# Two chained mixture-of-experts layers on one core: where the small steps of the second layer stand, four PSUM banks to a group of products, and weight addresses held in registers

## The chip, the core and the metric

The kernel runs on one core of a Trainium2 chip. TensorE (PE) multiplies, VectorE (DVE), ScalarE (ACT) and GpSimd (POOL) do the rest, SyncE (SP) issues most transfers. The metric is the device time of one launch in microseconds. Three runs of the kernel before took 2098.08, 2098.32 and 2103.15 us, so the median is 2098.32 us.

## The reference

Three stages follow each other on 14336 rows of 192 numbers.

```python
# 1: a causal convolution with softmaxed taps, one set of 7 for each of 8 heads of 24 columns
out = np.einsum('hk,bskhg->bshg', w, x_unf)
# 2: first layer, one expert of 8 for each row
expert_idx = np.argmax(x @ w_gate, axis=1)
h = np.maximum(xe @ w1[e], 0.0)             # (192, 1024)
out[mask] = gate_w[mask, None] * (h @ w2[e]) # (1024, 192)
# 3: second layer, two experts of 8 for each row, picked by noisy logits
noisy_logits = logits + np.log1p(np.exp(x @ w_noise)) * noise
out[mask] += top2_w[mask, k, None] * (h @ w2[e])
```

So the first layer puts 14336 rows through an expert, the second 28672. The kernel computes each float32 product as three 16-bit ones (high by high, high by low, low by high).

## The kernel before, in words

**Rows and steps.** The convolution and the gates run for 448 tokens at a time. POOL scatters each finished row into a table in DRAM (`rows1`, then `rows2`) that is ordered by expert. An expert's rows are then worked off in steps. A step is one expert and `t` rows: 1024 (two halves of 512 with the same weights), 512, 256 or 128. How many rows an expert gets is only known on the chip, so the number of steps of each size is fixed beforehand, and a table (`table`, one for each group of steps of one size) gives each step its expert and first row, as numbers that an engine loads into a register (`value_load`). The first layer has 68 steps: 45 of 256 rows, 2 of 512 and 21 of 128. The second has 77: 4 of 512 with their own copy of the second weights (the bridge, `tx`), 19 of 1024 as 38 halves, 7 of 512, 7 of 256 and 21 of 128. They stand in the order of `seq`: within a layer all large ones first, then 256, then 128. Steps share batches of up to 512 rows (`bats`) for their tiles `xT`, `ax`, `y`.

**A step** (`load`, `mm1`, `parts`, `mm2`, `finish`). SP loads 1 MB of first weights (`w1t`, three buffers), the step's rows transposed (`xT`, and for pairs `x3`) and their auxiliary columns (`ax`). `mm1` multiplies: for each of 8 chunks of 128 hidden columns there are four products with 128 contracted rows and one with 64 (192 = 128 + 64, and the low parts). With `st.nb == 2` two chunks in two banks are worked on together, and their two 64-row products run side by side in the upper and the lower half of the array. With `st.nb == 1` the fifth product uses 128 rows as well. `parts` empties a bank: ACT writes the rectified high half of `h`, DVE the low half. `mm2` multiplies `h` by the second weights `w2r` into a bank `py`, 24 products for each 128 rows. The weights are picked by the register `st.re` plus a constant, and the sequencer of PE computes that sum before each product. `finish` scales by the gate on ACT. In the second layer POOL then scatter-adds 128 rows to the output (`add_out`): the adds of one step don't wait for each other, but each waits for those of the step before.

**Order.** `run` goes through `seq`. It puts `mm1` of a step and `mm2` of the step before it in turns: one group of `nb` banks, then as many products of the second kind as keep step. All engines work their instructions in this written order. A planner with its own clocks (`pump`, `clk`) only decides where the other work (convolution, gates, row scatters) falls in between.

In the profile every instruction that goes through a small recording class has line 95.

Of the kernel before, what the change touches and what calls it, by code (L numbers as in the profile page):

```python
# [44 lines left out]
HOP = 0.15  # L45
BRIDGE = 4


# [4 lines left out]
def n_ceil(avail, t):  # L53
    return (avail + E * (t - 1)) // t
# [3 lines left out]
def conv_moe_moe2_kernel(ctx: ExitStack, tc: tile.TileContext, xh, cw, cwb, wg, w11, w21, w2t, w12, w22, out):  # L58
# [574 lines left out]
    def table(g, total):  # L633
# [48 lines left out]
        v.tensor_copy(tb[:, 0:2], val[:, 0:2])  # L682
        v.tensor_scalar(tb[:, 2:3], val[:, 1:2], float(FC * 2 * DG), None, op0=OP.mult)
        dg = L("dg", (P, 2, steps))
# [219 lines left out]
    def load(st):  # L904
# [16 lines left out]
        ins = [q_.dma_start_transpose(st.xT, rows[row, 0:HALF].bitcast(F16))]  # L921
        if st.nb == 2:
            if st.off == 0:
                st.b.x3 = wk.tile([P, 512], F16, name="x3", bufs=3)
            st.x3 = st.b.x3[:, st.off * P:st.off * P + T]
            ins.append(q_.dma_start_transpose(st.x3[:, None, :], rows[row, 32:96].bitcast(F16)))
# [5 lines left out]

    def chunk(st, k):

        n = 512 // st.T
        f, j = divmod(k, n)
        return f // st.nb * n + j + f % st.nb * FC // 2

    def mm1(st, f):


        T, n = st.T, 512 // st.T
        if f == 0:
            st.h = wk.tile([P, 2, 512 * FC // n], F16, name="h", tag="h", bufs=2)
            st.hv = st.h.rearrange("p k (c t) -> p k c t", c=FC)
        if f == st.nb % 2 and not st.g.own:
            st.re = t_.value_load(st.g.tb[st.i:st.i + 1, 2:3], min_val=0, max_val=(E - 1) * FC * 2 * DG)
        st.ph = [ps_h.tile([P, 512], F32, name="ph") for _ in range(st.nb)]
        x = lambda k: st.xT[:, k, :]
        for j in range(n):  # L950
            o = [ph[:, j * T:(j + 1) * T] for ph in st.ph]
            ws = []
            for b in range(st.nb):
                c = chunk(st, (f + b) * n + j)
                w = [st.w[0][:, k * F + c * P:k * F + (c + 1) * P] for k in range(4)]
                t_.matmul(o[b], w[0], x(0), start=True, stop=False)
                t_.matmul(o[b], w[0], x(2), start=False, stop=False)
                t_.matmul(o[b], w[1], x(0), start=False, stop=False)
                t_.matmul(o[b], w[2], x(1), start=False, stop=False)
                ws.append(w[3])  # L960
            if st.nb == 1:
                t_.matmul(o[0], ws[0], x(1), start=False, stop=True)
            else:
                t_.matmul(o[0], ws[0][:64], x(1)[:64], start=False, stop=True)
                t_.matmul(o[1], ws[1][64:], st.x3[64:], start=False, stop=True)

# [11 lines left out]

    w2flat = w2r.rearrange("p e c -> p (e c)")

    def mm2(st, lo, hi):

        for qn in range(lo, hi):
# [5 lines left out]
            hs = slice(s * P, (s + 1) * P)  # L989
            cw = chunk(st, c)  # L990
            if st.g.own:
                w = [st.w[1][:, (2 * cw + k) * D:(2 * cw + k + 1) * D] for k in range(2)]
            else:
                off = st.re + cw * 2 * dd
                w = [w2flat[:, bass.ds(off + k * dd if k else off, dd)] for k in range(2)]
            t_.matmul(py, st.hv[:, 0, c, hs], w[0], start=(c == 0), stop=False)
# [158 lines left out]
    def run(seq):  # L1155
# [12 lines left out]
        for n, st in enumerate(seq + [None]):  # L1168
# [9 lines left out]
            for f in range(0, ns, nb):  # L1178
                ahead(n + 3)
                if st is not None:  # L1180
                    clk["pe"] = max(clk["pe"], emptied[nb - 1])
                    mm1(st, f)
                    if st.g.m and f == ns - nb:
                        ahead(n + 4)
# [22 lines left out]

    def group(m, t, k, last, own, tag):
        g = Step()
        g.m, g.t, g.k, g.last, g.own, g.tag, g.tb, g.bc, g.deps = m, t, k, last, own, tag, None, None, None  # L1210
        for i in range(k):
            w = [None, None]
            for skip in range(0, t, 512):
                st = Step()
                st.g, st.T, st.i, st.skip, st.w, st.first, st.end = g, min(t, 512), i, skip, w, skip == 0, None
                st.nb = 2 if t > P and (m or t == 512) else 1
                S = st.T // P
                if not bats or bats[-1].S + S > 4:
                    bats.append(Batch())
                    bats[-1].S, bats[-1].pads = 0, False  # L1220
                st.b, st.off = bats[-1], bats[-1].S
                st.b.S += S
                st.b.pads |= last
                seq.append(st)
        return g

    def full_groups(m, left, sizes, tag):
# [9 lines left out]
    for k, n in enumerate(EPOCHS):  # L1237
        left, gs = full_groups(0, left + n * G * OT, (512, 256), f"ta{k}")
        if k == len(EPOCHS) - 1:
            gs.append(group(0, P, n_ceil(left, P), True, False, "ta"))  # L1240
        ep_groups.append(gs)
    n1, nb1 = len(seq), len(bats)
    bridge = group(1, 512, BRIDGE, False, True, "tx")
    left, rest = full_groups(1, 2 * N - BRIDGE * 512, (1024, 512, 256), "tb")
    rest.append(group(1, P, n_ceil(left, P), True, False, "tb"))

    def zero_out():
# [111 lines left out]
```

## Time and profile before

| what | value |
|---|---|
| median of three runs | 2098.32 us |
| the profiled execution, with what lies around its span | 2103.14 us |
| its span | 2101.1 us |
| PE busy | 1796.6 us (86%) |
| DVE, ACT, POOL busy | 946.8, 848.5, 834.3 us |
| mean granted clock of PE | 0.910 |

A granted clock of 1.00 is 2.4 GHz, 0.50 is 1.2 GHz. Matmuls are pipelined: one of 512 columns is shown as 0.38 us long while the next one starts much earlier. So a busy PE says little, and the distance from one start to the next is what counts. In a line of the order of time that merges n equal products, that distance is (its length less the length of one) / (n - 1). "Issue" is idle time for which the profile shows no one waited for.

### The profile page before, as it was taken

To read this page: it belongs to the slowest core of one execution; us is meant where nothing else is said; L and a number is where in the kernel's file an instruction comes from. 1 tells how busy PE (TensorE), PEld (TensorE's weight loads), DVE (VectorE), ACT (ScalarE), POOL (GpSimd) and SP (SyncE) were. 2 spreads that over 40 slices of the span, in tenths; PEclk is the share of its full clock that TensorE was granted. 3 is DMA by queue.
4 is the path that set the end of the run, shared out by engine and by line. 5 is a ranking of instruction groups with operands and counts; after the bars stand their busy time and mean duration, and the time that the engine had idled before them with its cause. 6 is when DMAs were issued, how large, how long until landed. Compare 5 with 4: busy or idle time off the path is not lost. (4 is left out here: it accounts for less than half of the span.)

```text
span 2101.1 us, 51695 instructions
## 1 busy us (share of the span) xinstructions
PE 1796.6 (86%) x16031; PEld 1365.3 (65%) x16031; DVE 946.8 (45%) x3508; ACT 848.5 (40%) x1756; POOL 834.3 (40%) x1512
## 2 busy tenths in 40 slices
PE   4778867667868897877789999999999999999993
PEld 3547756556757674766656666666666666667893
DVE  6856644535456574443345433333333333333341
ACT  4745644444334453433333333333333333333331
POOL 1453454545443334353335433333333333343323
PEclk9768988878879898888899999999999999999996
DMA  7868655334458785545698545554554556667792
GB/s 251 281 204 233 205 169 140 109 106 140 144 190 257 225 257 152 163 161 187 192 258 233 102 78 96 85 101 86 88 96 77 102 83 117 116 107 148 203 273 51
DMA packets 320693, 329.04 MB, mean 157 GB/s; under 512 B 230718, under 2 KB 279108, under 8 KB 303296
## 3 DMA queue, kind: packets, MB, share of 16 engines
q1 hardware_dynamic: 258400, 236.98, 40.2%
q0 software_dynamic: 55184, 74.92, 18.3%
q10 hardware_dynamic: 6864, 13.83, 2.0%
q8 instruction: 159, 2.61, 0.5%
q14 instruction: 86, 0.70, 0.1%
HBM read 189.50 MB, written 96.08 MB: 136 GB/s over the span
## 5 line engine op out<-in xcount | busy, mean ns | idle before, releaser
L95 PE MATMUL ph<-xT,w1t 128*128 128x256 f16 (+4 forms) x5568 | 877.0, 303 | 91.4 <-issue 78.7
L95 DVE SCALAR_TENSOR_TENSOR h<-ph,h 128x512 f16<-128x512 f32 x700 | 462.9, 687 | 961.1 <-ACT h L95 899.1
L95 PE MATMUL py<-w2r,h 128*128 x8016 | 813.5, 255 | 75.7 <-issue 74.4
L95 PEld LDWEIGHTS <-h 128*128 128x128 f16 x8400 | 726.2, 100 | 164.7 <-issue 146.8
L95 PEld LDWEIGHTS <-w1t 128*128 128x128 f16 (+1 forms) x5800 | 485.2, 101 | 398.0 <-issue 216.1
L95 ACT ACTIVATE h<-ph 128x512 f16<-128x512 f32 x700 | 392.3, 594 | 682.2 <-PE ph L95 493.7
L95 POOL DMA_INDIRECT out_dram<-y,ax x231 | 361.0, 1563 | 607.4 <-ACT y L95 421.3
L95 POOL DMA_INDIRECT rows<-row,gdi x238 | 237.3, 997 | 214.7 <-issue 189.0
L95 ACT ACTIVATE y<-py,cf 128x192 f32<-128x192 f32 (+1 forms) x350 | 148.6, 424 | 385.0 <-PE py L95 259.7
L95 POOL DMA_INDIRECT rows<-row,di x128 | 125.9, 984 | 152.2 <-DVE di L95 36.9
L95 POOL MEMSET spacer<- 1x1 f32 x613 | 172.4, 281 | 0.1
L95 PE MATMUL ph<-x,w1t 64*128 64x512 f16 (+1 forms) x232 | 87.3, 376 | 0.1
L95 PE MATMUL ph<-x,band 118*112 118x96 f32 x512 | 70.3, 299 | 5.2 <-issue 3.8
L95 PEld LDWEIGHTS ph<-x,band 118*112 118x112 f32 x512 | 66.4, 213 | 7.9 <-issue 5.5
L95 ACT ACTIVATE x<-x,ras 112x192 f32<-112x192 f32 x128 | 49.0, 446 | 19.3 <-DVE rai L95 13.2
L95 POOL CAST row<-gix 128x8 f32<-128x8 uint32 (+1 forms) x30 | 6.9, 229 | 110.0 <-DVE gex L95 47.0
L95 ACT ACTIVATE y<-y,rbs 128x192 f32<-128x192 f32 x119 | 46.5, 445 | 6.9 <-DVE rbs L95 6.9
L95 ACT ACTIVATE rT<-ph 128x672 f16<-128x672 f16 x64 | 43.2, 729 | 15.0 <-PE ph L95 10.7
L95 PE MATMUL ph<-ident,row 112*128 112x112 f16 x384 | 33.3, 245 | 15.4 <-DVE row L95 6.4
L95 PEld LDWEIGHTS <-row 112*128 112x128 f16 x384 | 27.6, 116 | 21.5 <-issue 12.7
L95 DVE TENSOR_TENSOR row<-x,row 112x256 f16<-112x256 f32 x64 | 33.4, 554 | 13.1 <-ACT row L95 12.9
L95 ACT ACTIVATE x<-ph 112x384 f32<-112x384 f32 x64 | 28.2, 480 | 27.0 <-PE ph L95 13.5
(275 smaller groups left out, 1142.6 us busy)
## 6 DMA issues: line engine op xcount, KB each, us to landing
w1t<-w1s SPq DMA_DIRECT2D x126, 1024.0 KB
x<-in_xh_dram ACTq DMA_DIRECT2D x32, 400.0 KB
w1raw<-in_w_dram SPq DMA_DIRECT2D x8, 1536.0 KB
w2raw<-in_w_dram SPq DMA_DIRECT2D x16, 768.0 KB
out_dram<-pads SPq DMA_DIRECT2D x11, 960.0 KB
w1s<-w1raw POOLq DMA_DIRECT2D x16, 512.0 KB
w1s<-whalf SPq DMA_DIRECT2D x16, 512.0 KB
w2tr<-in_w2t_dram POOLq DMA_DIRECT2D x16, 384.0 KB
```

Of the source, the lines that this page charges most:

```text
L95: r = f(*a, **kw)
```

## The change

Four things are changed.

- The second layer's steps of 256 and 128 rows are put into ten batches, and these stand between the large ones (`mixed`). Four large halves come first, and three steps of 512 rows end the program. In the last epoch of the first layer, two steps of 128 and one of 256 take turns (`packed`).
- In the second layer a group of steps with more than 128 rows takes all four banks `ph`: two chunks, then the 64-row products of all four, then the other two chunks. In the first layer the two steps of 512 rows take one bank at a time, and their fifth product uses 128 rows.
- At a step's third product PE loads the expert's offset once and adds 16 constants to it, in registers. Each second product then takes its address from a register.
- The chunks are worked off in plain order.

```diff
--- before.py
+++ after.py
...
         tb = cst.tile([P, 3], I32, name=g.tag + "tb")
         v.tensor_copy(tb[:, 0:2], val[:, 0:2])
-        v.tensor_scalar(tb[:, 2:3], val[:, 1:2], float(FC * 2 * DG), None, op0=OP.mult)
+        v.tensor_scalar(tb[:, 2:3], val[:, 1:2], float(4 * FC * DG), None, op0=OP.mult)
...
-        if st.nb == 2:
-            if st.off == 0:
+        if st.nb == 4:
+            if st.b.x3 is None:
                 st.b.x3 = wk.tile([P, 512], F16, name="x3", bufs=3)
...
     def mm1(st, f):
 
 
@@ -943,26 +938,45 @@
         if f == 0:
             st.h = wk.tile([P, 2, 512 * FC // n], F16, name="h", tag="h", bufs=2)
             st.hv = st.h.rearrange("p k (c t) -> p k c t", c=FC)
-        if f == st.nb % 2 and not st.g.own:
-            st.re = t_.value_load(st.g.tb[st.i:st.i + 1, 2:3], min_val=0, max_val=(E - 1) * FC * 2 * DG)
         st.ph = [ps_h.tile([P, 512], F32, name="ph") for _ in range(st.nb)]
         x = lambda k: st.xT[:, k, :]
+
+        def w(b, j, k):
+            c = (f + b) * n + j
+            return st.w[0][:, k * F + c * P:k * F + (c + 1) * P]
+
+        out_ = lambda b, j: st.ph[b][:, j * T:(j + 1) * T]
+        def whole(b):
+            for j in range(n):
+                o = out_(b, j)
+                first = j == 0 and b < 2
+                t_.matmul(o, w(b, j, 0), x(0), start=first, stop=False, skip_group_check=True)
+                t_.matmul(o, w(b, j, 0), x(2), start=False, stop=False, skip_group_check=True)
+                if f == b == j == 0 and not st.g.own:
+                    addresses(st)
+                t_.matmul(o, w(b, j, 1), x(0), start=False, stop=False, skip_group_check=True)
+                t_.matmul(o, w(b, j, 2), x(1), start=False, stop=b > 1, skip_group_check=True)
+
+        if st.nb == 4:
+            whole(0)
+            whole(1)
+            for b in (0, 2):
+                for j in range(n):
+                    for i, (rows, src) in enumerate(((slice(0, 64), x(1)), (slice(64, P), st.x3))):
+                        t_.matmul(out_(b + i, j), w(b + i, j, 3)[rows], src[rows], start=b == 2 and j == 0,
+                                  stop=b == 0, skip_group_check=True)
+            whole(2)
+            whole(3)
+            return
         for j in range(n):
-            o = [ph[:, j * T:(j + 1) * T] for ph in st.ph]
-            ws = []
-            for b in range(st.nb):
-                c = chunk(st, (f + b) * n + j)
-                w = [st.w[0][:, k * F + c * P:k * F + (c + 1) * P] for k in range(4)]
-                t_.matmul(o[b], w[0], x(0), start=True, stop=False)
-                t_.matmul(o[b], w[0], x(2), start=False, stop=False)
-                t_.matmul(o[b], w[1], x(0), start=False, stop=False)
-                t_.matmul(o[b], w[2], x(1), start=False, stop=False)
-                ws.append(w[3])
-            if st.nb == 1:
-                t_.matmul(o[0], ws[0], x(1), start=False, stop=True)
-            else:
-                t_.matmul(o[0], ws[0][:64], x(1)[:64], start=False, stop=True)
-                t_.matmul(o[1], ws[1][64:], st.x3[64:], start=False, stop=True)
+            o = out_(0, j)
+            t_.matmul(o, w(0, j, 0), x(0), start=True, stop=False)
+            t_.matmul(o, w(0, j, 0), x(2), start=False, stop=False)
+            if f == j == 0 and not st.g.own:
+                addresses(st)
+            t_.matmul(o, w(0, j, 1), x(0), start=False, stop=False)
+            t_.matmul(o, w(0, j, 2), x(1), start=False, stop=False)
+            t_.matmul(o, w(0, j, 3), x(1), start=False, stop=True)
...
-    w2flat = w2r.rearrange("p e c -> p (e c)")
+    w2bytes = w2r.rearrange("p e c -> p (e c)").bitcast(mybir.dt.uint8)
+
+    def addresses(st):
+
+        pe = nc.tensor
+        first = pe.value_load(st.g.tb[st.i:st.i + 1, 2:3], min_val=0, max_val=4 * (E - 1) * FC * DG)
+        step = 2 * (D if st.g.m else DG)
+        st.wr = []
+        for k in range(2 * FC):
+            r = pe.alloc_register(f"w2at{len(addressed)}_{k}")
+            pe.reg_alu(r, first, W2_AT + k * step, op=OP.add)
+            st.wr.append(pe.snap(r, min_val=W2_AT, max_val=W2_AT + 4 * (E - 1) * FC * DG + k * step,
+                                 guaranteed_mod_val=0, out_of_modulus=32))
+        addressed.append(st)
+
+    addressed = []
...
-            cw = chunk(st, c)
+            cw = c
             if st.g.own:
                 w = [st.w[1][:, (2 * cw + k) * D:(2 * cw + k + 1) * D] for k in range(2)]
             else:
-                off = st.re + cw * 2 * dd
-                w = [w2flat[:, bass.ds(off + k * dd if k else off, dd)] for k in range(2)]
+                w = [w2bytes[:, bass.ds(st.wr[2 * cw + k] - W2_AT, 2 * dd)].bitcast(F16) for k in range(2)]
...
-                    clk["pe"] = max(clk["pe"], emptied[nb - 1])
+                    clk["pe"] = max(clk["pe"], emptied[nb // 3])
...
-                st.nb = 2 if t > P and (m or t == 512) else 1
+                st.nb = 4 if m and t > P else 1
...
+    def queue(parts_):
+
+        for st in parts_:
+            S = st.T // P
+            if not bats or bats[-1].S + S > 4 or bats[-1].m != st.g.m:
+                bats.append(Batch())
+                bats[-1].S, bats[-1].pads, bats[-1].m, bats[-1].x3 = 0, False, st.g.m, None
+            st.b, st.off = bats[-1], bats[-1].S
+            st.b.S += S
+            st.b.pads |= st.g.last
+            seq.append(st)
+
+    def in_order(groups):
+        for g in groups:
+            while g.steps:
+                queue(g.steps.popleft())
+
+    def mixed(groups, first, after):
+
+        large = deque(p for g in groups if g.t >= 512 for p in g.steps)
+        small = []
+        for g in groups:
+            if g.t < 512:
+                while g.steps:
+                    small.append([st for _ in range(min(512 // g.t, len(g.steps))) for st in g.steps.popleft()])
+            g.steps.clear()
+        for _ in range(first):
+            queue(large.popleft())
+        n, k = len(small), len(large) - after
+        for i in range(k):
+            for b in small[i * n // k:(i + 1) * n // k]:
+                queue(b)
+            queue(large.popleft())
+        while large:
+            queue(large.popleft())
+
+    def packed(groups):
+
+        by = {g.t: g.steps for g in groups}
+        big, mid, low = by.get(512, deque()), by.get(256, deque()), by.get(P, deque())
+        while mid and len(low) >= 2:
+            for _ in range(2):
+                queue(low.popleft())
+            queue(mid.popleft())
+            if big and len(mid) % 3 == 1:
+                queue(big.popleft())
+        in_order(groups)
 
...
             gs.append(group(0, P, n_ceil(left, P), True, False, "ta"))
+            packed(gs)
+        else:
+            in_order(gs)
...
     bridge = group(1, 512, BRIDGE, False, True, "tx")
+    in_order([bridge])
     left, rest = full_groups(1, 2 * N - BRIDGE * 512, (1024, 512, 256), "tb")
     rest.append(group(1, P, n_ceil(left, P), True, False, "tb"))
+    mixed(rest, 4, 2)
```

On PE, inside a large step of the second layer, the end of a group before (`ph` are banks, `x3` marks the lower half of a pair, `py` is the second product):

```order
L95 LDWEIGHTS w1t_18105
L95 MATMUL ph_18819<-xT_18322,w1t_18105 128x512
L95 LDWEIGHTS w1t_18105
L95 MATMUL ph_18818<-xT_18322,w1t_18105 128x512
L95 LDWEIGHTS w1t_18105
L95 MATMUL ph_18819<-x3_18325,w1t_18105 128x512
L95 LDWEIGHTS h_18593
L95 ISA
L95 MATMUL py_18830<-w2r_128,h_18593 128x192
```

and the middle of a group now:

```order
L96 LDWEIGHTS w1t_20841
L96 MATMUL ph_21525<-xT_20843,w1t_20841 128x512
L96 LDWEIGHTS w1t_20841
L96 MATMUL ph_21524<-xT_20843,w1t_20841 128x512
L96 LDWEIGHTS w1t_20841
L96 MATMUL ph_21525<-x3_20846,w1t_20841 128x512
L96 LDWEIGHTS w1t_20841
L96 MATMUL ph_21526<-xT_20843,w1t_20841 128x512
L96 LDWEIGHTS w1t_20841
L96 MATMUL ph_21527<-x3_20846,w1t_20841 128x512
L96 LDWEIGHTS w1t_20841
L96 MATMUL ph_21526<-xT_20843,w1t_20841 128x512
```

Two pairs of 64-row products now stand behind each other, between full products on both sides, and the register instruction (ISA) ahead of each `py` product is gone.

On PE, the start of a large step before:

```order
L95 LDWEIGHTS h_18367
L95 ISA
L95 MATMUL py_18769<-w2r_128,h_18367 128x192
L947 TENSOR_LOAD tb1024tb_17237
L947 ISA x2
L95 LDWEIGHTS w1t_18105
L95 MATMUL ph_18818<-xT_18322,w1t_18105 128x512
```

and now:

```order
L96 MATMUL ph_21524<-xT_20843,w1t_20841 128x512
L998 TENSOR_LOAD tb1024tb_20456
L998 ISA x2
L96 LDWEIGHTS w1t_20841
L1003 ISA
L1004 ISA
L1003 ISA
L1004 ISA
L1003 ISA
L96 MATMUL ph_21524<-xT_20843,w1t_20841 128x512
```

The value load moved from the step's first product to its third, and five instructions of fused register arithmetic follow it there. In the steps with one bank it stood ahead of the second bank's products before.

On SP, the last loads of the program before (`tbtb` is the table of the 128-row steps):

```order
L908 TENSOR_LOAD tbtb_17837
L908 ISA x2
L910 TENSOR_LOAD tbtb_17837
L910 ISA x2
L95 ISA
L95 DMA w1t_30848<-w1s1_84 128x4096
L95 ISA
L95 DMA_TRANSPOSE xT_30621<-rows2_82 128x3x128
```

and now (`tb512tb` is that of the 512-row steps):

```order
L909 TENSOR_LOAD tb512tb_20630
L909 ISA x2
L911 TENSOR_LOAD tb512tb_20630
L911 ISA x2
L96 ISA
L96 DMA w1t_37112<-w1s1_84 128x4096
L96 ISA
L96 DMA_TRANSPOSE xT_37114<-rows2_82 128x3x512
```

The last steps had 128 rows each and now have 512. Up to the last epoch of the first layer the order of all else on the five engines is as before.

## Rows read from the trace of the kernel before

**Rows 1.** Busy time by stretch: stretch, length, each engine (count), granted clock, DMA share, GB/s.

```profile
152.80:781.80 629.00, 484.97 (x4475) 418.52 (x4475) 346.86 (x1639) 296.07 (x639) 259.74 (x593) 0.84 0.61 181
781.80:1080.50 298.70, 236.87 (x2327) 194.62 (x2325) 133.02 (x580) 112.00 (x245) 119.73 (x264) 0.86 0.59 181
...
1146.80:1896.90 750.10, 748.55 (x6124) 498.00 (x6122) 259.54 (x527) 270.87 (x540) 294.83 (x374) 1.00 0.55 95
1896.90:1966.20 69.30, 67.68 (x666) 54.12 (x665) 21.57 (x50) 21.92 (x44) 25.54 (x32) 1.00 0.69 154
1966.20:2066.70 100.50, 97.66 (x1395) 91.65 (x1392) 39.65 (x106) 34.56 (x66) 27.69 (x35) 1.00 0.89 237
2066.70:2101.10 34.40, 0.00 (x0) 0.00 (x0) 0.00 (x0) 0.42 (x1) 10.59 (x13) 0.54 0.19 21
```

**Rows 2.** PE in order of time, one group of a large step: start, length, what.

```profile
1302.11 1.89 PE L95 MATMUL ph<-xT,w1t 128*128 128x512 f16 x8
...
1303.94 0.39 PE L95 MATMUL ph<-x,w1t 64*128 64x512 f16 x1
1304.26 2.15 PE L95 MATMUL py<-w2r,h 128*128 x24
1306.25 1.89 PE L95 MATMUL ph<-xT,w1t 128*128 128x512 f16 x8
```

**Rows 3.** PE in order of time, the first step of 256 rows.

```profile
1896.94 1.25 PE L95 MATMUL ph<-xT,w1t 128*128 128x256 f16 x9
1897.91 0.28 PE L95 MATMUL ph<-x,w1t 64*128 64x256 f16 x1
...
1899.31 4.96 PE L95 MATMUL py<-w2r,h 128*128 x48
```

**Rows 4.** A step of 128 rows: PE in order of time, its sequencer's value load.

```profile
1983.71 1.15 PE L95 MATMUL py<-w2r,h 128*128 x12
1985.09 1.29 PE L95 MATMUL ph<-xT,w1t 128*128 128x128 f16 x20 [0.23 <-issue]
...
L947 PEldq TENSOR_LOAD <-tbtb x1: 308/308/308, 1984.4 to 1984.4; - x1
```

**Rows 5.** PE's sequencer by line: ns min/median/max, first and last start; PE's product at 1146.80.

```profile
L947 PEldq FUSED_REGOPS  x141: 151/151/165, 155.1 to 2061.2; - x141
...
L95 PEldq FUSED_REGOPS  x8: 46/46/46, 1300.1 to 1301.0; - x8
...
L947 PEldq TENSOR_LOAD <-tb1024tb x38: 297/303/407, 1145.3 to 1762.7; - x38
...
1146.80 0.38 PE L95 MATMUL ph<-xT,w1t 128*128 128x512 f16 x1
```

**Rows 6.** Busy time by stretch during a burst of row scatters, first layer.

```profile
1009.00:1011.00 2.00, 0.99 (x9) 0.46 (x7) 0.00 (x0) 0.00 (x0) 1.81 (x5) 1.00 0.96 371
1011.00:1013.00 2.00, 0.22 (x1) 0.19 (x2) 0.00 (x0) 0.00 (x0) 1.57 (x5) 1.00 1.03 159
1013.00:1015.00 2.00, 0.60 (x3) 0.23 (x3) 0.00 (x0) 0.00 (x0) 1.78 (x4) 0.95 0.23 73
1015.00:1017.00 2.00, 0.79 (x5) 0.24 (x3) 0.00 (x0) 0.00 (x0) 1.00 (x2) 0.50 0.18 66
```

**Rows 7.** PE's last products and POOL's scatter-adds, in order of time.

```profile
1906.04 1.56 POOL L95 DMA_INDIRECT out_dram<-y,ax  x1 [0.27 <-issue]
...
2063.76 2.90 PE L95 MATMUL py<-w2r,h 128*128 x22
...
2066.15 1.56 POOL L95 DMA_INDIRECT out_dram<-y,ax  x1 [2.70 <-issue]
...
2092.53 1.56 POOL L95 DMA_INDIRECT out_dram<-y,ax  x1 [3.32 <-issue]
```

**Rows 8.** The costliest groups: DVE empties a bank (busy, mean ns, idle before).

```profile
L95 DVE SCALAR_TENSOR_TENSOR h<-ph,h 128x512 f16<-128x512 f32 x700 | 462.9, 687 | 961.1 <-ACT h L95 899.1
```

**Rows 9.** PE in order of time, a 256-row step of the first layer around its value load.

```profile
866.94 1.25 PE L95 MATMUL ph<-xT,w1t 128*128 128x256 f16 x10
```

More of the change, by code (lines that the diff above doesn't have):

```diff
@@ L46 @@
 BRIDGE = 4
+W2_AT = 20480
 def n_full(avail, t):
@@ L931, in load @@
         st.at = clk["done"]
[L933 to L937, printed above, removed]
     def mm1(st, f):
@@ L1210, in group @@
         g.m, g.t, g.k, g.last, g.own, g.tag, g.tb, g.bc, g.deps = m, t, k, last, own, tag, None, None, None
+        g.steps = deque()
         for i in range(k):
             w = [None, None]
+            parts_ = []
             for skip in range(0, t, 512):
@@ L1215, in group @@
                 st.g, st.T, st.i, st.skip, st.w, st.first, st.end = g, min(t, 512), i, skip, w, skip == 0, None
-                st.nb = 2 if t > P and (m or t == 512) else 1
[L1217 to L1224, printed above, removed]
-        return g
+                st.nb = 4 if m and t > P else 1
+                parts_.append(st)
+            g.steps.append(parts_)
+        return g
+    def queue(parts_):
[39 more added lines that the diff above has]
+        in_order(groups)
     def full_groups(m, left, sizes, tag):
```

## The prediction

> **What bounds the kernel now.** I read the busy time by stages first. In it look at PE's busy time, its granted clock and the DMA share side by side. From 153 to 1080 us, the first layer, PE works 485 of 629 us and 237 of 299 us at a mean clock of 0.84 and 0.86. From 1147 to 1897 us it works 748.6 of 750.1 us at clock 1.00. In the small steps at the end it still works 97.7 of 100.5 us, with the DMA engines at 0.89. In the last 34.4 us it does nothing [rows 1]. So the second layer is bound by PE, and the end by something after PE.
>
> Next comes PE's order of time in one group of a large step (two banks, eight full products, one pair of 64-row products, 24 products of the second matmul). Eight full products follow each other at (1.89 - 0.38) / 7 = 0.216 us. From the first to the pair they should take 1.73 us and take 1.83. The pair should hold PE for 0.216 us and the next product starts 0.32 us behind it [rows 2]. So each visit to 64 rows costs 0.10 us on entry and 0.10 on exit, and the period of 4.14 us is otherwise at its pitch (24 products at (2.15 - 0.25) / 23 = 0.0826 us). Register arithmetic costs nothing there. It shows where 48 products of the second matmul stand in a run: 4.96 us, a pitch of 0.100 instead of 0.0826 [rows 3].
>
> In the 128-row steps I looked at the start of a step. The value load and its check hold PE's sequencer from 1984.4 to about 1985.09, 0.69 us. Twelve products of 0.99 us became 1.38 us, with 0.23 us marked as issue [rows 4].
>
> Last, the end. PE is done at 2063.76 + 2.90 = 2066.66. The last scatter-add starts at 2092.53, and the span ends 8.6 us later, at 2101.1. Seven adds start from 2066.15 on, (2092.53 - 2066.15) / 6 = 4.40 us apart, each waiting for the one before [rows 7]. The 21 steps of 128 rows give one such add each, so the adds fall behind while the DMA engines are full.
>
> Up to 1080 us the cause of the idle time is another one. While POOL scatters rows of the first layer's output, PE gets few instructions through: busy 0.60 of 2 us at 1013, with the DMA engines at 0.23. The clock falls to 0.50 by the end of it [rows 6]. Such a burst is eight scatters, four blocks of rows to two places each.
>
> **The change, part by part.** The sums are on the profiled execution (2103.1 us with what lies around its span of 2101.1). It is 4.8 us above the median of 2098.3, and I take the difference over to the median.
>
> *Order of the second layer.* The ten batches of small steps go between large ones and three large steps end the program. A 512-row step issues four adds in some 16 us of PE. Only the first of them waits for the step before: the one at 1906.04 starts 0.27 us after the one before it, so 1.56 + 0.27, some 1.9 us, is the pitch without a wait [rows 7]. At worst a large step needs 4.4 + 3 x 1.9 = 10 us of POOL, so what four small steps leave behind is caught up in the next large one. The last add should start about 1 us after PE's end (one activation and the issue, an estimate), and the 8.6 us behind it stay: 34.4 becomes 9.6, **-24.9 us**. What is late next is PE itself. Each moved step takes its three DMAs along on SP. The 1 MB weight load of a small step still waits for a buffer that comes free two steps earlier; that sufficed at 4.5 us a step, and now the neighbours are longer. I add nothing for it, up to 1.5 us per batch (+15) as a bound.
>
> *Four banks.* A large step visits 64 rows twice instead of four times: 2 x 0.21 = 0.41 us for each of 49 steps, **-20.3 us**. No row shows two pairs in a row. From below, the second pair follows at 0.216 us as full products do. From above, it pays one more 0.10 us, +12 in all (98 groups, and 21 pairs in the 256-row steps). I take the first, since loads of full weights hide behind a running product [rows 2]. Banks: the first two of a group are closed in its middle, DVE needs 4 x 0.69 = 2.8 us for four [rows 8], and the next group starts 4 us after this one's end. That cover is gone only where the step before is small (1 us of second products), and there the first two banks still have half a group.
>
> *Addresses in registers.* One register instruction per second product goes, and five longer ones come at each step's third product. Nothing changes in the large steps, where the 24 products kept their pitch [rows 2]. It is what lets 48 stand in a row at 0.0826. Small steps, at the pitches of the rows: seven of 256 rows, 7 x 4.12 (32 full and 4 pairs at 0.109, one visit) + 384 x 0.0826 = 60.6 instead of 69.3; 21 of 128 rows, 840 x 0.0563 + 552 x 0.0826 = 92.9 instead of 100.5. That is 16.3 us.
>
> The price is the sequencer's pause: 0.69 us, and five fused instructions at 0.046 to 0.151 us and some 0.06 between them, so 1.2 to 1.75 us [rows 4, 5]. Queued behind it are the step's own products. What covers it is what PE already has queued: where the preceding products needed no registers, the value load started at 1145.3, 1.5 us ahead of the product behind it [rows 5]. With two products of the new step among those queued I get 1.3 us of cover (128 rows) to 1.7 (512). So 0 to 0.45 us shows per small step. I take 0.1 for 28 steps: 16.3 - 2.8, **-13 us**. In the large steps I take 0.
>
> *First layer.* Up to about 780 us only the register instructions differ. A 256-row step there has no gap at the value load [rows 9], so nothing to win; its 128-row steps give 21 x 0.15 = 3. The two 512-row steps lose the pairing and its switches, near zero. In the mixed last epoch the batches and bursts stay as many. **-2 us**, between -15 and +15, for the bursts fall on other steps.
>
> Sum: -24.9 - 20.3 - 13 - 2 = -60. The profiled 2103 becomes 2043, the median 2098.3 becomes **2038 us**.
>
> **Rivals.**
> *The second pair hides nothing* (0.17): 119 x 0.10 = +12, 2050 us. For it: both edges of every visit show 0.10 us [rows 2]. Against it: those are changes of shape, and between the two pairs there is none. The Trainium skill has the rule for this one ("TensorE: Matmul & The Clock Gate", Part 3, The mechanism): a weight load overlaps running products only when its row group differs, and the second pair uses the row groups of the first. The trace does not bear the rule out for full rows, where loads in one row group hide at a pitch of 0.216 us; for 64 rows no run shows it yet.
>
> *The pause shows* (0.10): 0.45 us at 42 steps of 128 rows, 0.3 at 52 of 256, 0.05 at 45 of 512, 37 us instead of about 4: 2071 us. For it: the 0.23 us already marked as issue [rows 4]. Against: with one instruction in three gone the sequencer runs further ahead.
>
> *The first layer's stalls shorten* (0.06): PE idles 144 + 62 = 206 us up to 1080 [rows 1]. Were these stalls a matter of instructions waited for, a fifth fewer of them would save some 40 us: 1998. Against: each stall ends with its burst.
>
> *Slower* (0.04): the adds now come in pairs, and behind a batch of small steps in a queue. If POOL then stops PE as the row bursts do, 5.4 us idle out of 8 and half clock behind it [rows 6], some 7 us each, nine such stalls cancel the gain; one behind each of the ten small batches and one in the last steps gives 77 us, 2115. For it: POOL runs them back to back. Against: the two adds 1.9 us apart at 1906 left no idle time beyond the stretch's 1.6 us [rows 1, 7].
>
> *Forecast* (0.58): 2038, between 2028 and 2048. The remaining 0.05 is a mixed order that waits for weights or costs time in the first layer (2055 to 2100).
>
> **How the numbers follow.** About 0.3%, 6 us, is what can be told from no change. Faster gets all but the slower rival and a cent or two of the rest: 0.94, same 0.02, slower 0.04. The range runs from 2016, half way to the case of shorter stalls, to 2068, which holds the second pair at full price with the late weights, and leaves out most of the pause's case and the slower one.
>
> **What would show it.** PE's last product and the last add about 1 us apart instead of 26. A large step in 16.1 instead of 16.6 us, and within a group the two pairs 0.22 us apart (right) or 0.32 (the rival). Second products at 0.083 us in runs of 48 and 96. No issue time over 0.1 us at the value loads. The first 780 us within some 10 us of before. I am wrong if PE waits for weights or banks between batches of different size, or if PE's idle time appears beside the adds.

## The result and the profile after

The changed kernel took 2030.3 us (median of 2026.1, 2029.6, 2031.0 and 2050.9) beside 2098.6 for the kernel before: ratio 0.969, 95% interval 0.962 to 0.976. Forecast were 2038 us within 2016 to 2068. The profiled execution took 2031.0 us, its span 2029.3. The sum was nearly right, but two of its four terms were not, and their errors cancelled for the most part.

Busy time by stretch in the changed kernel: start and end, length, then PE, weight loads, DVE, ACT and POOL with their counts, granted clock, DMA share, GB/s. The stretches are the first layer up to its last epoch, the last epoch, the first five steps of the second layer, the rest of it, and what follows PE's end.

```profile
153.20:769.50 616.30, 481.52 (x4475) 413.57 (x4475) 347.06 (x1639) 296.29 (x639) 261.06 (x594) 0.87 0.61 183
769.50:1053.20 283.70, 226.54 (x2327) 192.78 (x2326) 134.25 (x591) 111.53 (x245) 122.92 (x264) 0.90 0.65 193
1053.20:1143.40 90.20, 81.26 (x628) 52.73 (x626) 50.13 (x218) 32.02 (x65) 48.33 (x83) 0.94 0.84 211
1143.40:2018.00 874.60, 868.43 (x8042) 636.96 (x8040) 310.66 (x635) 332.12 (x637) 341.81 (x429) 1.00 0.61 119
2018.00:2029.30 11.30, 0.02 (x1) 0.00 (x0) 0.00 (x0) 0.42 (x1) 3.79 (x5) 0.68 0.28 29
```

Against [rows 1] the two parts of the first layer fell from 629.0 and 298.7 us, by 27.7 together, where I had given 2. The same cut in the trace of before gives 84.6 us for the first five steps, 901.6 for the rest and 34.4 for the tail, so these moved by +5.6, -27.0 and -23.1. With 0.4 us of a later start that is the 71.8 us between the two spans.

One group of a large step, PE in order of time, and two runs of second products nearer the end:

```profile
1272.56 2.23 PE L96 MATMUL ph<-xT,w1t 128*128 128x512 f16 x9
1274.40 0.39 PE L96 MATMUL ph<-x,w1t 64*128 64x512 f16 x1
1274.62 0.38 PE L96 MATMUL ph<-xT,w1t 64*128 64x512 f16 x1
1274.62 0.38 PE L96 MATMUL ph<-x,w1t 64*128 64x512 f16 x1
1274.93 1.90 PE L96 MATMUL ph<-xT,w1t 128*128 128x512 f16 x8
...
1997.92 4.12 PE L96 MATMUL py<-w2r,h 128*128 x48
...
2005.98 12.04 PE L96 MATMUL py<-w2r,h 128*128 x144
```

The second pair starts 0.22 us behind the first, and only the next full product comes 0.31 later: one switch for two pairs, as forecast. The Trainium skill has a rule by which a weight load overlaps running products only when its row group differs ("TensorE: Matmul & The Clock Gate", Part 3, The mechanism). For that case my rival had 0.32; the trace has 0.22 and does not bear the rule out. 48 second products now stand at (4.12 - 0.25) / 47 = 0.0823 us, where [rows 3] had 0.100, and 144 do so as well.

A 128-row step, PE in order of time, and below it PE's sequencer by line (ns min/median/max, first and last start):

```profile
1619.37 1.15 PE L96 MATMUL py<-w2r,h 128*128 x12
1620.36 0.28 PE L96 MATMUL ph<-xT,w1t 128*128 128x128 f16 x2
1620.92 1.16 PE L96 MATMUL ph<-xT,w1t 128*128 128x128 f16 x18 [0.29 <-issue]
1621.92 1.15 PE L96 MATMUL py<-w2r,h 128*128 x12
```

```profile
L998 PEldq TENSOR_LOAD <-tbtb x21: 296/303/384, 1604.0 to 1955.7; - x21
...
L1003 PEldq FUSED_REGOPS  x423: 105/160/186, 154.1 to 1994.1; - x141
```

Here the forecast failed. The third product comes 0.51 us behind the second instead of 0.06. From the start of the value load to the end of the last addition the sequencer is busy 1.7 us, the top of my 1.2 to 1.75. Seventeen products were queued ahead (three of the bank before, twelve second products, the step's own two): 1.2 us. Between others of its kind such a step takes 4.54 to 4.80 us, in [rows 4]'s kernel 4.42 to 4.62.

The end, POOL's last scatter-adds, with ACT's scaling of the last step's first 128 rows between them:

```profile
2010.84 1.56 POOL L96 DMA_INDIRECT out_dram<-y,ax  x1 [0.38 <-ACT y L96]
2012.17 0.42 ACT L96 ACTIVATE y<-py,cf 128x192 f32<-128x192 f32 x1 [1.61 <-PE py L96]
2015.16 1.56 POOL L96 DMA_INDIRECT out_dram<-y,ax  x1 [2.72 <-ACT y L96]
...
2020.76 1.56 POOL L96 DMA_INDIRECT out_dram<-y,ax  x1 [0.27 <-issue]
```

PE ends at 2005.98 + 12.04 = 2018.02. The last step's four adds stand 1.87 us apart, and the last starts 2.7 us behind PE, not 25.9 as in [rows 7]. The rows of the first of the four were ready at 2012.59, but it starts 4.32 us behind the last add of the step before, for which it has to wait.

### The profile page after: what moved, and what is told of

The parts are those of the page before. It is cut to its first block, busy times and chain, and to the rows that moved or that the text cites. A ratio compares the mean times of both kernels' runs of the same rounds, so it can differ in the third digit from the quotient of the medians.

```text
span 2029.3 us, 44327 instructions
## 1 busy us (share of the span) xinstructions
PE 1757.0 (87%) x16031; PEld 1365.2 (67%) x16031; DVE 947.2 (47%) x3520; ACT 860.3 (42%) x1756; POOL 839.3 (41%) x1512
## 4 chain that ended last, share of the span: by engine, by line
PE 53%; issue 3%; DVE 1%; POOL 0%; ACT 0%; another core or an unknown queue 0%; POOLq 0%
PE ph L96 27%; PE py L96 26%; POOL out_dram L96 0%; DVE h L96 0%; PE pr L96 0%; ACT y L96 0%; ACT h L96 0%; ACT row L96 0%; DVE tbtk L96 0%; POOL spacer L96 0%; DVE tbcm L96 0%; DVE row L96 0%; DVE gix L96 0%; DVE cf L96 0%
## 5 line engine op out<-in xcount | busy, mean ns | idle before, releaser
L96 PE MATMUL ph<-xT,w1t 128*128 128x256 f16 (+3 forms) x5576 | 863.4, 300 | 91.8 <-issue 81.8
L96 PE MATMUL py<-w2r,h 128*128 x8016 | 786.2, 254 | 62.8 <-issue 59.7
L96 PEld LDWEIGHTS <-h 128*128 128x128 f16 x8400 | 737.5, 100 | 121.5 <-issue 79.5
L96 PEld LDWEIGHTS <-w1t 128*128 128x128 f16 (+1 forms) x5800 | 472.4, 100 | 388.5 <-issue 216.1
L96 ACT ACTIVATE h<-ph 128x512 f16<-128x512 f32 x700 | 403.9, 595 | 543.5 <-PE ph L96 373.4
L96 PE MATMUL ph<-x,w1t 64*128 64x512 f16 (+1 forms) x224 | 63.8, 369 | 2.1 <-issue 2.1
L96 PE MATMUL ph<-ident,row 112*128 112x112 f16 x384 | 31.7, 237 | 12.6 <-ACT x L96 5.9
L96 PEld LDWEIGHTS <-row 112*128 112x128 f16 x384 | 26.0, 111 | 18.6 <-issue 14.6
```

The source lines that it names most:

```text
L96: r = f(*a, **kw)
```

## The experiments

The runs came in five groups, each beside runs of the kernel before. In two of them the kernel before took 1848 and 1849 us, not 2078 to 2098. So kernels are compared within a group, or by stage where the stage was the same everywhere. These two groups ran on two chips, the two with e8 to e12 on a third; no run separates the chip from the time. All lengths of stages in us, cut as above:

| kernel | beside, us | median | first layer | last epoch | five steps | rest | tail |
|---|---|---|---|---|---|---|---|
| before, first profile | | 2098.6 | 629.0 | 298.7 | 84.6 | 901.6 | 34.4 |
| changed, first profile | 2098.6 | 2030.3 | 616.3 | 283.7 | 90.2 | 874.6 | 11.3 |
| e1 changed | 1849.3 | 1801.6 | 483.1 | 207.2 | 76.3 | 874.9 | 11.3 |
| e2 spread additions | 1849.3 | 1776.2 | 463.4 | 203.6 | 77.9 | 862.3 | 11.2 |
| e3 old order, 2nd layer | 1849.3 | 1825.3 | 472.7 | 208.3 | 76.4 | 876.1 | 34.6 |
| e4 old order, last epoch | 1849.3 | 1800.4 | 485.6 | 207.0 | 76.4 | 875.0 | 11.4 |
| e5 before | 1848.1 | 1843.4 | 471.0 | 199.5 | 79.5 | 901.9 | 39.1 |
| e6 before + registers | 1848.1 | 1853.7 | 476.3 | 205.7 | 79.5 | 906.3 | 39.1 |
| e7 changed, two banks | 1848.1 | 1828.3 | 478.7 | 208.4 | 77.8 | 897.8 | 11.3 |
| e8 changed, no registers | 2078.5 | 2077.2 | 610.2 | 297.4 | 89.2 | 922.6 | 9.3 |
| e9 before + spread registers | 2078.5 | 2053.9 | 590.0 | 284.9 | 82.4 | 886.4 | 41.4 |
| e10 changed | 2097.8 | 2036.9 | 614.4 | 291.1 | 93.7 | 874.5 | 11.2 |
| e11 spread additions | 2097.8 | 2016.2 | 609.5 | 291.2 | 89.9 | 862.9 | 11.3 |
| e12 old order, last epoch | 2097.8 | 2040.8 | 616.8 | 294.8 | 93.4 | 874.8 | 11.4 |

**The kernels themselves again (e1, e5, e10: no edit).**

> The changed kernel once more. In its first profile the first layer (first product of the first step to the first product of the second layer) took 1053.2 - 153.2 = 900.0 us, before the change 927.7 us; I had given it 2 us, not 27.7. Theory A (the change shortens the stalls under row scatters): 900 us again, within 8, and a median of 2026 to 2032 us. Rival B (the stalls differ by chance from run to run): anything from 890 to 930 us in this profile, and single runs that spread over 20 us or more.

> The kernel before, unchanged, for its profile next to the others. In the four runs before this one the kernel before took 1849 us, not 2098, and the changed kernel 1801.6. The second layer of the changed kernel took the same in both (874.6 and 874.9 us from its sixth step to PE's end, tail 11.2), its first layer 690.3 us instead of 900.0. Theory: what made the 250 us is in the stalls beside POOL's row scatters alone and not in this kernel's code, so here too the second layer of the kernel before takes 901.6 us (within 1), its tail 34.4, and all the difference is in the first layer, 680 to 700 us. With 51 us gained in the second layer and the tail and 47.8 in all, its first layer should then be about 4 us shorter than the changed kernel's 690. Rival (the gain of 27.7 us in the first layer is the change's doing): first layer 715 us or more here.

> The changed kernel once more, next to the two below. Where the kernel before takes some 2078 to 2098 us (stalls beside the row scatters), the first layer of the changed kernel was 27.7 us shorter in one pair of profiles; where it takes 1848 us, it was 20 us longer. Theory (two effects: the pause costs 13 to 20 us in the first layer, and where PE stalls, the pause lies in the stall and the missing register instructions save time): if the kernel before takes 2070 to 2100 us here, the changed one is 60 to 72 us faster, with a first layer of 875 to 900 us; if it takes 1848 us, 45 to 50 us faster, first layer 682 to 693. Rival (the first pair of profiles differed by chance): 30 to 45 us faster beside a kernel before of 2070 to 2100 us, first layer as long as that of the kernel before or longer (900 to 925 us).

e1 against its group: ratio 0.974 (0.971 to 0.977); e10: 0.971 (0.968 to 0.975), 60.9 us. e5 is the kernel before itself (1.0005). The rest of the second layer repeats within 0.4 us in every group where a kernel ran again, 0.6 with spread additions. The first layer does not. e5 and e1 show what it is without the stalls, the kernel before first:

```profile
150.40:621.40 471.00, 428.04 (x4475) 398.60 (x4475) 347.07 (x1638) 293.94 (x639) 264.37 (x593) 0.94 0.83 239
621.40:820.90 199.50, 195.17 (x2326) 175.82 (x2324) 134.45 (x583) 112.72 (x247) 123.95 (x265) 1.00 0.97 268
```

and the changed kernel:

```profile
148.80:631.90 483.10, 434.90 (x4475) 402.54 (x4475) 347.85 (x1639) 296.65 (x639) 266.59 (x594) 0.93 0.81 234
631.90:839.10 207.20, 195.77 (x2327) 179.12 (x2325) 136.06 (x593) 112.91 (x247) 123.23 (x265) 1.00 0.88 254
```

The change makes the first layer 19.8 us longer there, 690.3 for 670.5 (some 12 by subtraction of the other stages from the medians' 47.7 us). With the stalls it is shorter: 905.5 us in e10, 900.0 in the first profile, 927.7 before. Neither theory of e1 held as written, since the amount hangs on the stalls; that of e10 held, but for 5 us more than its 900. e5's theory held for the rest (901.9), but not for the tail (39.1 for 34.4) and the first layer (670.5 for 680 to 700); its rival, 715, falls.

A stall in e10, PE in order of time, the brackets idle time and its end; then the same burst's scatters on POOL:

```profile
1010.66 0.74 PE L96 MATMUL ph<-xT,w1t 128*128 128x128 f16 x6
1012.62 0.22 PE L96 MATMUL ph<-xT,w1t 128*128 128x128 f16 x1 [1.21 <-issue]
1013.35 0.22 PE L96 MATMUL ph<-xT,w1t 128*128 128x128 f16 x1 [0.51 <-issue]
1014.79 0.22 PE L96 MATMUL ph<-xT,w1t 128*128 128x128 f16 x1 [1.22 <-issue]
```

```profile
1011.94 0.98 POOL L96 DMA_INDIRECT rows<-row,gdi  x1 [0.18 <-issue]
1013.23 0.97 POOL L96 DMA_INDIRECT rows<-row,gdi  x1 [0.23 <-issue]
```

And such a burst in e1, the same program, PE and then POOL:

```profile
810.05 1.23 PE L96 MATMUL py<-w2r,h 128*128 x12
811.12 1.28 PE L96 MATMUL ph<-xT,w1t 128*128 128x128 f16 x20
812.24 1.23 PE L96 MATMUL py<-w2r,h 128*128 x12
```

```profile
809.69 0.97 POOL L96 DMA_INDIRECT rows<-row,gdi  x1 [0.23 <-issue]
810.97 0.97 POOL L96 DMA_INDIRECT rows<-row,gdi  x1 [0.23 <-issue]
```

The scatters are equally long and equally far apart. In one group PE gets an instruction every 0.7 or 1.4 us beside them, in the other it works on at its pitch.

**The pause (e2, e11).** The value load stays; the additions go two by two to each chunk's third product.

```diff
-                if f == b == j == 0 and not st.g.own:
-                    addresses(st)
+                addresses(st, (f + b) * n + j)
...
-        for k in range(2 * FC):
+        for k in range(2 * c, 2 * c + 2):
```

> The changed kernel, with the value load where it is, but the sixteen address additions two by two at the third product of each of the eight chunks instead of all at the first. Theory: the 0.3 us gap behind the second product of a 128-row step is the part of value load plus five fused instructions (about 1.3 to 1.7 us) that the queue ahead (about 1.3 us) does not cover. With 0.8 us in one place it is covered: 128-row steps between others of their kind go from 4.55 to 4.70 us to about 4.25, 256-row steps lose 0.26 us each, the second layer about 21 x 0.40 + 7 x 0.26 = 10 us shorter, some 2020 us in all. Rival 1 (the value load alone makes the gap, because its check lets the queue run dry): gap stays 0.29 us and the time within 3 us of the kernel it is made from. Rival 2 (eight pieces of register work slow every chunk): no gap, but 128-row steps stay above 4.5 us.

> The changed kernel with spread additions, again, next to the changed kernel on one chip. Theory: second layer 862 us on any chip, 12.5 us less than the changed kernel. Where PE stalls beside the row scatters the pause is hidden in the first layer, so 12 to 18 us faster than the changed kernel; where it doesn't, 25 us as before. Rival (the pause costs the first layer the same everywhere): 25 us in either case.

Ratios 0.962 (0.959 to 0.965) and 0.961 (0.958 to 0.963): 25.3 and 20.7 us less than the changed kernel beside it, and the fastest of all in either group. PE in a 128-row step of e2:

```profile
1600.79 2.97 PE L96 MATMUL py<-w2r,h 128*128 x34
1603.60 1.28 PE L96 MATMUL ph<-xT,w1t 128*128 128x128 f16 x20
```

The gap is gone, twenty products follow at 0.0558 us, and these steps take 4.21 us. The second layer's rest is 12.6 us shorter (forecast 10). Both rivals of e2 fall. Of what is left, by subtraction from the medians, some 14 us lie in the first layer without stalls (23.3 in the profiles, but e2's was the fastest of its six runs) and in e11 some 5. That points to a pause that lies in the stalls there, as theory said, though 20.7 stands between its 12 to 18 and the rival's 25, with single runs 9 to 22 us apart.

**Registers alone (e6, e9) and all but registers (e8).** e6 is the kernel before with `addresses(st)` at the third product, e9 with e2's spread. e8 is the changed kernel with

```diff
-                w = [w2bytes[:, bass.ds(st.wr[2 * cw + k] - W2_AT, 2 * dd)].bitcast(F16) for k in range(2)]
+                off = st.re + cw * 2 * dd
+                w = [w2flat[:, bass.ds(off + k * dd if k else off, dd)] for k in range(2)]
```

> The kernel before with the address registers alone (value load and sixteen additions at the third product of a step; two banks, old order of steps). Theory: in the second layer the large steps gain the 0.07 us by which they shrank more than the switches account for (8.70 to 8.64 us beside their second products), 256-row steps fall from 9.9 us by about 0.5, 128-row steps stay as they are (what 24 products gain at 0.083 us the pause takes), so some 6 us less in the second layer. In the first layer the pause costs 0.25 us in 45 steps of 256 rows and 0.4 in 21 of 128, less what the products gain there: 5 to 15 us more. In all within 8 us of the kernel before. Rival (one instruction in three gone from PE's second products frees PE where it is starved): 15 us or more faster than the kernel before, with the first layer shorter.

> The kernel before with address registers alone, the sixteen additions two by two at the third product of each chunk (two banks, old order). Theory: without the pause the registers are worth what I gave them: 128-row steps 2.64 to 2.23 us beside their second products (-8.6), large steps without their 0.14 us at the value load (-6), 256-row steps -4: the second layer 883 us instead of 901.9, the first layer 665 to 670 us like the changed kernel with spread additions (667.0) and the kernel before (670.5). In all about -20 us, 1828 us. Rival 1 (first layer and pause have nothing to do with each other: the changed first layer is longer for another reason): first layer 680 us or more. Rival 2 (spread additions slow the chunks): 128-row steps stay at 2.5 us.

> The changed kernel with the old addressing: the value load at the third product stays, but no address registers; each second product's address is added up just before it. Theory (my step: registers are what lets 48 second products stand in a row at 0.083 us): each run of 48 takes 4.96 us as in the first 256-row step of the kernel before, 1.0 us more; some 5000 second products of the second layer behind value-loaded weights make 105 such runs, +100 us; the pause goes, -10 to -30 us. In all 1870 to 1895 us where the changed kernel takes 1801.6 and the kernel before 1848: slower than before. Rival (PE's queue is long enough for 48): runs of 48 at 4.0 to 4.3 us, 1775 to 1800 us.

e6: ratio 1.004 (1.002 to 1.006), 0.4% slower. The 256-row steps gained 0.27 us each, the 128-row ones lost 0.10, and the large ones lost 0.10, which no theory had. Their value load holds PE too. PE in e6, a group without value load and the next one with it, and below them the value loads of the large steps in e6 and in the changed kernel (ns min/median/max):

```profile
1056.38 2.21 PE L96 MATMUL ph<-xT,w1t 128*128 128x512 f16 x9
...
1060.52 2.44 PE L96 MATMUL ph<-xT,w1t 128*128 128x512 f16 x9
```

```profile
L985 PEldq TENSOR_LOAD <-tb1024tb x38: 299/488/597, 891.3 to 1510.9; - x38
...
L998 PEldq TENSOR_LOAD <-tb1024tb x38: 297/303/484, 1118.5 to 1837.7; - x38
```

Seventeen products are queued ahead of them in either kernel, for 1.51 us; but in e6 the load takes 0.49 us where it takes 0.30 in the changed kernel, and what doesn't fit under the queue shows. Why it is longer there was not found.

e9: ratio 0.989 (0.986 to 0.993), 24.6 us faster; the second layer's rest 15.5 us shorter than in e5: 7.5 in the 128-row steps, 3.9 in those of 256 and 4.1 in the large ones, which lose the 0.09 us that the old value load held them. That this is near my 16.3 is chance, since the 16.3 were for small steps alone and held some 4.5 us of fewer 64-row visits; the terms for the small steps fit. e8: 0.999 (0.996 to 1.001): without registers the whole change is worth nothing. I had expected 22 to 47 us more than the kernel before. PE in e8:

```profile
1290.45 4.19 PE L96 MATMUL py<-w2r,h 128*128 x48
...
1299.16 10.96 PE L96 MATMUL py<-w2r,h 128*128 x95
```

A run of 48 behind a large step's products is nearly covered (4.19 us, within the rival's 4.0 to 4.3); the 96 ahead of a small step are not (some 11.0 instead of 8.0). In all +48 us in the rest (922.6 for 874.6), half of what I expected, and as much as order and banks bring. Part of it lies at the value loads: with the old addressing PE has 1 to 3 products queued there (medians of the three sizes), not seventeen.

**Order and banks (e3, e4, e12, e7).** One line each; e7 also fits the loops over the banks to it:

```diff
-    mixed(rest, 4, 2)
+    in_order(rest)
...
-            packed(gs)
+            in_order(gs)
...
-                st.nb = 4 if m and t > P else 1
+                st.nb = 2 if m and t > P else 1
```

> The changed kernel with the second layer's steps in the old order (all large ones, then 256, then 128 rows). Theory: the tail behind PE's end is back at about 34 us from 11.3, nothing else changes in the second layer: +23 us, about 2053 us. Rival (the scatter-adds of 128-row steps are slowed by what stands beside them, and the registers or banks shortened the tail too): tail of 20 us or less and 2040 us. Rival 2: the small steps run faster next to each other (their weights come in time in either order, but the first of a batch of 128 rows takes 0.3 us more than its products): +15.

> The changed kernel with the first layer's last epoch in the old order (two steps of 512, seven of 256, then twenty-one of 128 rows). The last epoch took 298.7 us before and 283.7 us after. Theory A (the turns of 128, 128 and 256 rows gave most of it): it is back at 295 to 300 us, the time 10 to 15 us longer. Rival B (fewer PE instructions gave it, or chance): 280 to 288 us and the time within 5 us of the changed kernel.

> The changed kernel with the first layer's last epoch in the old order, again, next to the changed kernel. Where PE didn't stall the order was worth nothing (-1.1 us). Theory (the order spreads the row scatters, whose stalls cost time only where PE stalls): if the kernel before takes 2070 to 2100 us, 5 to 15 us slower than the changed kernel, the last epoch at 290 us or more; if it takes 1848 us, within 3 us. Rival (the order is worth nothing anywhere): within 5 us in either case.

> The changed kernel with two banks to a group in the second layer: 64-row products after every two chunks, four times in a 512-row step instead of twice. Theory: 0.41 us more in each of 49 large steps and 0.2 in each of 7 of 256 rows, +21.5 us, 1823 us where the changed kernel takes 1801.6; a large step's part beside its second products goes from 8.23 to 8.64 us. Rival (only part of the 0.477 us per large step came from the banks, the rest from registers or the order of chunks): less than +15 us. Rival 2 (four banks made PE wait for emptied banks somewhere): less than +15 as well, with idle time in front of a group's first product in the changed kernel.

e3 is 23.7 us slower than e1, and its tail is 34.6: the theory. e4 is 1.2 us faster (difference of means -0.6, give or take 5), e12 3.8 slower (2.8, give or take 9): the order of the last epoch is worth nothing that could be measured. e12's expectation of 5 to 15 us is not borne out, but not excluded up to some 12. e7 is 26.7 us slower than e1 across two groups with the same kernel before, 22.9 of it in the rest: theory, 21.5. Its rivals had less than 15. The large steps came to 8.71 us, not 8.64, since with two banks the value load shows in them: with spread additions two banks have 8.61 (e9) and four 8.19 (e2), so 0.42 of the 0.48 are the banks'.

## Why the prediction was right or wrong, point by point

**Order, -24.9: right.** -23.1 in the profile, 23.7 by e3. It was 1.8 us less since the last add starts 2.7 us behind PE, not 1. My sum had left out that the last step's first add, too, waits for the step before: it comes 4.32 us after that one, and the other three, back to back at 1.87, don't catch up. Late weights, my bound of +15, cost nothing; no idle time stands ahead of a batch.

**Four banks, -20.3: right.** A large step less 0.0826 us for each second product takes 8.61 us with two banks and 8.19 with four where no pause shows (e9, e2): 0.42 for my 0.41. In the change it fell from 8.70 to 8.23, -21.0 us in 44 steps, of which the banks are some 18.6; the rest is the old value load (0.09 us a step) less the new pause (0.05). No run changes the order of the chunks by itself. The rival of a second pair at full price falls by the 0.22 us.

**Addresses in registers, -13: wrong in size.** The second layer's small steps moved by -6.9 us (256 rows) and +0.9 (128 rows), -6.0 in all, and some 4.5 of that are the 64-row visits of the 256-row steps, which my term held too. By themselves (e6) the registers cost 4.4 us in the rest and 5 us or more in all. The step that failed is "I take 0.1 for 28 steps" and "In the large steps I take 0". For the small steps rows gave bounds of 0 to 0.45, and I chose near the lower end. Measured (e2 against e1) are 0.42 in 128-row steps, 0.25 in 256-row ones and 0.05 in large ones, 12.6 us where I took 2.8. Without the pause the term was well sized: in e2 the small steps are 16.6 us shorter than before, for my 16.3. The argument against my rival, that the sequencer runs further ahead with fewer instructions, was true and not enough: ahead of the value load of a 128-row step five products were queued before and seventeen now (medians), but never more than seventeen in any run, and these last 1.2 to 1.4 us there against 1.75 us of register work.
What I did not count at all is that the registers carry the other parts. Without them (e8) the rest is 21.0 us longer than before, although its fewer 64-row visits are worth some 23; so, by subtraction, the longer runs of second products that four banks and the mixed order make cost some 44 us.

**First layer, -2: wrong both ways.** My step looked only for what there was to win at the value load and put no price on the pause there. Where PE does not stall, the pause costs it: +19.8 in the profiles and some 12 by the medians, and e2 wins back all of it (23.3 and some 14). Where PE stalls, it gained 22 to 28 us. That was the rival of shorter stalls, with 40 us; the mechanism would fit, at half to two thirds of the size. Instructions come in one by one there, and one in three of the second products' is gone. Taking the stages' differences from the medians (stages of the kernel before from its first profile), the first layer of e8, with the old number of instructions, gained some 2 us, and that of e9 some 10 to 14. This is by subtraction, good to 5 to 10 us, and so points to the instructions without settling it; the order of the epoch is excluded only beyond some 12 us (e12). The cause of the gain stays open.

**Slower by stopped PE: no.** PE has 868.4 us of work in 874.6, and no stall stands beside the scatter-adds there.

**Open:** the first five steps of the second layer became 6 to 9 us longer where PE stalls, and 3 shorter where not. The last burst of scatters falls on another step there. It is not the registers (89.2 us in e8 without them, 82.4 in e9 with them and little else) nor the order of the epoch (93.4 in e12); the other parts of the change were not separated, and these are single profiles.

So 2038 came out near 2030 and, in e10, nearer still to 2037 by luck: errors cancelled, 10 us of pause too little in the second layer and 8 to 11 in its first five steps, against 20 (e10) to 26 too little gained in the first layer.

## What to carry to other kernels

Put register work on a sequencer next to what its engine has queued, in microseconds of that very stretch, and cut the block where it is longer: eight pieces of 0.1 us showed nowhere on PE where one block of 1.7 cost 21 to 25 us in all. Where a price is bounded by rows from both sides, the middle is a better choice than the end that suits the forecast. A stage with unexplained idle time needs its own range, in both directions, however little of the change falls in it.

## What the runs showed of the hardware that was not expected

- The same program takes 12% less in some groups of runs than in others (before 1848 to 2098 us, changed 1802 to 2037), nearly all of it in stages with row scatters. Starts on PE, its weight loads and register work 0.6 to 0.8 us behind the one before number some 200 in the first layer of the first profile, 160 in the changed one, and 3 in e1; but 183 in e9, whose first layer was shorter than the changed one's, so the count alone doesn't give the time. Other engines stand still too: in the burst of e10 at 1010 ACT is idle for 8.79 us, waiting for a signal of PE. The scatters take 0.97 us, 1.28 apart, in either case. What decides between the two was not found.
- Two pairs of 64-row products in the same row groups follow each other at 0.22 us, like full products.
- A value load takes 0.30 us, its check lasts until about 0.7, and sixteen additions end at 1.7 us. PE runs on for seventeen queued products, 1.2 to 1.5 us by their width, and never had more queued at a value load in any of the runs. With the old addressing it had five ahead of the 128-row steps' value loads (median).
